# Paired diagonal turns, paired weight turns, and another order in the first units of a block, in the backward pass of a gated attention and feed-forward mix

## The chip, the core and the metric

The kernel runs on one core of a Trainium2 chip. The core has a matrix engine (TensorE, PE in the profile, with its weight loads shown as PEld), a vector engine (DVE), an activation engine (ACT), a general engine (POOL) and SyncE (SP), which here only issues DMAs. Each engine works through its own list of instructions in order and waits for the others on semaphores. Sixteen DMA engines move data between device memory and the on-chip memory, and they also turn (transpose) tiles on the way. The metric is the device time of one execution in microseconds (us). Three runs of the kernel before took 967.56, 969.1 and 969.56 us; the median is 969.1.

## The reference, cut to what matters

The forward pass mixes two branches with a gate per row. Branch A is attention with 32 heads of 16 columns over 2048 positions, in which each query sees itself and the 255 positions before it. Branch B is a gated feed-forward layer.

```python
qkv = (x @ wqkv).reshape(B, S, 3, H, Dh) ...          # S 2048, D 512, H 32, Dh 16
mask = (idx[:, None] - idx[None, :] >= 0) & (idx[:, None] - idx[None, :] < 256)
p = softmax(where(mask, q k^T * Dh ** -0.5, -1e9))
a = (p @ v) @ wo
b = ((x @ W_gate) * (x @ W_gate > 0) * (x @ W_up)) @ W_down        # F 1376
g = sigmoid((x * gate_w).sum(-1, keepdims=True))
out = g * a + (1 - g) * b
```

The kernel returns `out` and, for a given `grad_out`, the gradients of x, wqkv, wo, W_gate, W_up, W_down and gate_w, in bfloat16.

## The kernel before

The kernel has three stages. The first (0 to about 258 us) runs the feed-forward layer forward and backward and writes its intermediate results to device memory. The second (about 258 to 771 us) is attention, forward and backward. The third (to the end at 964 us) multiplies the stored results by turned weights and gives `out` and the gradient of x. The change touches the second stage, and the turned weights that the second stage loads for the third.

**Units.** The 32 heads are cut in four column chunks `c` of 128 columns, that is eight heads each. The 2048 positions are cut in 16 blocks of 128. For each chunk and each query block `j` the window reaches over the key blocks `j-2`, `j-1` and `j`. Such a pair of blocks is handled for four heads at a time (`half` 0 or 1), and that is one unit. A block has six units, block 0 has two and block 1 has four, so that there are 360 units in all. The role of a unit is `d` (diagonal, the key block is the query block), `m` (middle) or `f` (far). In a full block the order is m, f, d of the first half and then m, d, f of the second. The first unit of a block is thus an m unit of the first half, except in block 0.

**One unit.** `front` makes the scores ST on PE (L611), takes the exponential into `Pu` on ACT (L617) and masks it on POOL for d and f units (L619, L622). `front_dp` makes dPT on PE (L631), `gradp` multiplies it into `Pd` on DVE (L636). Three units later (`LAG = 3`) `rowsum` multiplies `Pu` and `Pd` into the accumulator BA on PE (L645, L647); after the last unit of a block ACT copies BA out (L651) and `small_ops` on DVE and POOL finish the block's rows. BA has one buffer. `flip` turns `Pu` and `Pd` into `p2`: d units and m units of the first half by a DMA that SyncE issues (L659), two units after `front`; the other units by eight PE transposes (L668) into PSUM and a copy by ACT or DVE in turn (L72, L74), three units after `front`. In the last chunk the last two blocks (`c == DC - 1`, `j >= NT - 2`) are turned by PE alone. `cd_piece` later multiplies the turned tiles by the finished rows into the accumulator CD (L486, L489), which ACT copies out (L492); these pieces wait in the list `cdq` with the number of the unit from which they may run.

**Order of the work.** The loop `while n <= NU + LAG` writes out the order by hand, one turn of the loop per unit `n`. PE gets ST of unit n, the row sums of unit n-3 (L820), the PE transposes of unit n-3, dPT of unit n (L836), one or two CD pieces (L838 to L840) and, where a running budget `credit` allows, a part of the next projections or of the gradient of wqkv. The scores, dPT, projections and weight gradients share four PSUM buffers (tag `M`). SyncE gets the turns of unit n-2, then weights, stores and the copies `z` that spread projected rows, in the order of the loop.

**Buffers.** `PP` (six buffers) holds `Pu` and `Pd` of a unit that is turned by DMA or is diagonal; `Pu` and `Pd` (four each) those of the other units. The turned tiles have seven buffers for d, seven for m and four for f.

**Turned weights.** `plan` lists what is loaded for the third stage while attention runs. `turns` gives one DMA for each 128 columns of wqkv, W_gate and W_up (`turn_w`, L516), 34 in all, and the loop issues one in every three units.

## Time and profile before

| | us |
|---|---|
| median of three runs | 969.1 |
| the profiled execution | 966.0 |
| its span, first to last instruction | 964.3 |
| 0 to 258, PE busy | 251.73 of 258 |
| 258 to 771, PE busy | 492.67 of 513 |
| the same stretch, DVE, ACT and POOL busy | 344.16, 353.56 and 336.21 |
| 771 to 964.3, PE busy | 187.78 of 193.3 |
| granted TensorE clock, mean | 0.993 |

The page gives busy times by engine, the chain of work that ended last, and groups of instructions by source line. A group's line reads: line, engine, operation, what it writes and reads, shape, number, busy time, mean duration in ns, idle time of the engine just before these instructions, and what ended that idle time. Matmuls are pipelined: each is drawn longer than the distance at which the next can start, so that short waits of PE do not show as idle time. A timeline shows instructions in order of time (start, duration, engine, line, operation). For a DMA the issue on its queue and the landing are told apart.

SyncE issues the DMA turns of attention as `DMA_TRANSPOSE` instructions. The turns of PP (128x1024 elements) land a median of 3.8 us after their issue, at least 3.0; the turns of the first stage's `hT` (128x512) a median of 2.8, at least 2.3. The seven large turns of the third stage land a median of 8.6 us after their issue.

### The profile page before, as it was taken

The numbers are of one execution on the slowest core, as the hardware profiler recorded it, in microseconds if no ns is written. First come the engines' busy times: TensorE is split into PE (matmuls) and PEld (weight loads), VectorE is DVE, ScalarE is ACT, GpSimd is POOL, SyncE is SP. The second block draws the span as 40 slices with busy tenths as digits, with TensorE's granted clock in tenths as the row PEclk, the third lists the DMA queues.
The fourth block names the chain that finished last, engine by engine and source line by source line (L and its number), as shares of the span: only waits on it lengthen the run. The fifth ranks groups of instructions, "written<-read, shape, count | busy, mean of one in ns | idle before, by whom it ended". The sixth has DMA issues, their size and how long they took to land.

```text
span 964.3 us, 27296 instructions
## 1 busy us (share of the span) xinstructions
PE 932.2 (97%) x11065; PEld 589.3 (61%) x11065; DVE 504.1 (52%) x921; ACT 457.8 (47%) x795; POOL 486.8 (50%) x935
## 2 busy tenths in 40 slices
PE   8999999999989999999999999979998999999998
PEld 5556556566557766677776776756766744444443
DVE  4433435334467776567775767756676432223223
ACT  5522322223367877667776677756676410000001
POOL 1645445455177667656676656755666521112211
PEclk9999999999999999999999999989999999999999
DMA  9988799999579797987979869998999699787741
GB/s 286 191 188 192 184 199 213 198 215 207 133 123 141 112 178 127 135 159 115 175 126 147 156 105 172 135 149 140 167 139 199 148 260 228 193 189 190 188 106 44
DMA packets 473399, 160.32 MB, mean 166 GB/s; under 512 B 402008, under 2 KB 470968, under 8 KB 473272
## 3 DMA queue, kind: packets, MB, share of 16 engines
q1 hardware_dynamic: 450872, 135.49, 76.6%
q10 hardware_dynamic: 20592, 17.84, 6.5%
q0 software_dynamic: 1808, 5.24, 1.6%
q8 instruction: 86, 1.41, 0.6%
q14 instruction: 41, 0.34, 0.2%
HBM read 32.15 MB, written 36.31 MB: 71 GB/s over the span
## 4 chain that ended last, share of the span: by engine, by line
PE 82%; POOL 5%; DMA 4%; DVE 4%; issue 2%; ACT 1%; SPq 1%; POOLq 0%; DVEq 0%; ACTq 0%
PE wps L371 7%; PE dxps L952 7%; PE pt L668 7%; PE ST L611 7%; PE dPT L631 7%; PE dxps L967 4%; PE wps L568 4%; PE BA L645 4%; PE pp L128 4%; PE dhps L324 4%; PE ups L324 4%; PE dps L373 4%; PE bps L921 3%; PE gps L324 3%; PE CD L486 3%
## 5 line engine op out<-in xcount | busy, mean ns | idle before, releaser
L636 DVE TENSOR_TENSOR PP<-PP,dPT 128x512 bf16<-128x512 bf16 x186 | 126.2, 681 | 51.5 <-POOL PP L619 46.4
L636 DVE TENSOR_TENSOR Pd<-Pu,dPT 128x512 bf16<-128x512 bf16 x174 | 118.0, 679 | 63.5 <-POOL Pu L622 47.9
L631 PE MATMUL dPT<-z,V 128*128 128x512 bf16 x360 | 137.1, 381 | 9.3 <-ACT PP L617 7.6
L617 ACT ACTIVATE PP<-ST 128x512 bf16<-128x512 f32 x186 | 112.0, 602 | 67.5 <-PE ST L611 50.7
L611 PE MATMUL ST<-z,K 128*128 128x512 bf16 x360 | 136.9, 380 | 4.8 <-DVE PP L636 1.4
L617 ACT ACTIVATE Pu<-ST 128x512 bf16<-128x512 f32 x174 | 105.3, 605 | 45.7 <-PE ST L611 35.9
L619 POOL TENSOR_SCALAR_AFFINE_SELECT PP<-PP 128x512 bf16<-128x512 bf16 x128 | 81.5, 637 | 79.2 <-ACT PP L617 78.3
L338 POOL TENSOR_TENSOR hT<-rg,upm 128x512 bf16<-128x512 bf16 x44 | 51.5, 1170 | 119.0 <-DVE upm L336 91.8
L486 PE MATMUL CD<-rq,p 128*128 128x32 bf16 x1440 | 109.6, 177 | 0.7 <-ACT rows_st L492 0.5
L489 PEld LDWEIGHTS <-p 128*128 128x128 bf16 x1440 | 86.3, 96 | 35.5 <-issue 2.4
L489 PE MATMUL CD<-rq,p 128*128 128x16 bf16 x1440 | 106.7, 169 | 0.0
L371 PE MATMUL wps<-dgu_r,x_r 128*128 128x256 bf16 x704 | 105.6, 273 | 0.4 <-DVE wst L74 0.4
L486 PEld LDWEIGHTS <-p 128*128 128x128 bf16 x1440 | 98.9, 96 | 10.7 <-issue 8.5
L72 ACT COPY p<-pt 128x1024 bf16<-128x1024 bf16 x89 | 90.7, 1019 | 4.8 <-PE pt L668 1.2
L371 PEld LDWEIGHTS <-x_r 128*128 128x128 bf16 x704 | 68.8, 98 | 31.7 <-issue 1.0
L622 POOL TENSOR_SCALAR_AFFINE_SELECT Pu<-Pu 128x512 bf16<-128x512 bf16 x112 | 71.2, 635 | 28.9 <-ACT Pu L617 27.3
L930 ACT COPY a_sb<-aps 128x512 f32<-128x512 f32 x16 | 9.4, 586 | 153.1 <-issue 137.6
L336 DVE SCALAR_TENSOR_TENSOR upm<-rg,ups 128x512 bf16<-128x512 bf16 x44 | 30.1, 684 | 80.0 <-PE ups L324 40.3
L330 ACT ACTIVATE rg<-gps 128x512 bf16<-128x512 f32 x44 | 26.3, 598 | 89.1 <-PE gps L324 44.1
L668 PE MATMUL pt<-ident,Pd 128*128 128x128 bf16 x696 | 67.8, 220 | 0.0
L668 PE MATMUL pt<-ident,Pu 128*128 128x128 bf16 x696 | 67.1, 218 | 0.1
L373 PE MATMUL dps<-db_r,h_r 128*128 128x512 bf16 x176 | 66.7, 379 | 0.0
(159 smaller groups left out, 2033.7 us busy)
## 6 DMA issues: line engine op xcount, KB each, us to landing
dqkvo_d<-rows_st SPq DMA_DIRECT2D x7, 1024.0 KB, 6.4
hT_d<-hT ACTq DMA_DIRECT2D x44, 128.0 KB, 2.3
dgT_d<-dgu ACTq DMA_DIRECT2D x44, 128.0 KB, 2.9
duT_d<-dgu ACTq DMA_DIRECT2D x44, 128.0 KB, 2.9
duT_g<-duT_d SPq DMA_DIRECT2D x8, 640.0 KB, 5.4
gt<-hT_d SPq DMA_DIRECT2D x7, 640.0 KB, 5.3
dgT_g<-dgT_d SPq DMA_DIRECT2D x7, 640.0 KB, 5.2
z<-zT SPq DMA_DIRECT2D x60, 64.0 KB, 2.2
```

Source lines behind the costliest of these rows:

```text
L72: nc.scalar.copy(out, in_)
L324: nc.tensor.matmul(out[:], lhsT=w(c), rhs=x(c), start=(c == 0), stop=(c == DC - 1))
L371: nc.tensor.matmul(acc["w"][:, c, :], lhsT=x_r[:, t, c * P:(c + 1) * P], rhs=k.dgu_r[:, :, i, :], start=(go_ and c % 2 == 0), stop=no_, sk ...
L373: nc.tensor.matmul(acc["d"][:], lhsT=k.h_r[:, i, :], rhs=db_r[:, t, :], start=go_, stop=no_)
L486: nc.tensor.matmul(cd[0][:, h, :], lhsT=p2[:, 0, hh, :], rhs=rq[:, h, 0:2 * Dh], start=cd[1], stop=True, skip_group_check=True)
L489: nc.tensor.matmul(cd[0][:, h, 0:Dh], lhsT=p2[:, 1, hh, :], rhs=rq[:, h, 2 * Dh:3 * Dh], start=False, stop=True, skip_group_check=True)
L611: nc.tensor.matmul(ST[:], lhsT=KTt[:, ksl], rhs=z[:, 0, jl, :, :], start=True, stop=True)
L617: nc.scalar.activation(u.Pu[:], ST[:], ACT.Exp)
L619: nc.gpsimd.affine_select(out=u.Pu[:], in_=u.Pu[:], compare_op=ALU.is_ge, fill=0.0, base=0, pattern=[[0, HH], [1, P]], channel_multiplier=-1)
L631: nc.tensor.matmul(u.dPT[:], lhsT=VTt[:, ksl], rhs=z[:, 1, jl, :, :], start=True, stop=True)
L636: nc.vector.tensor_tensor(out=u.Pd[:], in0=u.Pu[:], in1=u.dPT[:], op=ALU.mult)
L668: nc.tensor.transpose(pt[:, a, hh, :], src[:, hh, :], ident[:])
```

## The change

- The two diagonal units of a query block share one tile `PPd`, and after the second one a single DMA of 128x2048 elements turns both. Before, each had a DMA of its own, the first one two units after its own `front`.
- The buffers change with that: `PPd` has two buffers of double size and `PPm` three, in place of six of `PP`; `Pu` and `Pd` have three for four; the turned pairs `P2d` have four (of two units each) for seven of one, and the turned m tiles six for seven.
- The exception for the last two blocks of the last chunk is gone: their d units and the m units of the first half are turned by DMA too. That takes six of the 178 PE turns away and adds two pairs and two single DMA turns.
- Weights are turned two column blocks at a time, 18 DMAs in place of 34.
- In the loop turn in which the row sums of a block's first unit come up, PE gets dPT of unit n and the CD piece (or pieces) ahead of these row sums. In all other turns the order stays.

Counted over the program, SyncE issues 64 turns of pairs and 60 of single units in place of 182 turns, and 18 of weights in place of 34.

```diff
-        def turn_w(name, src, k, tag, at):
-            piece_of(name, k, tag, at)
-            r0 = min(k * P, src.shape[1] - P)
-            nc.sync.dma_start_transpose(out=W6[(name, k)], in_=src[:, r0:r0 + P])
+        def turn_w(name, src, ks, tag, at):
+            for i, k in enumerate(ks):
+                piece_of(name, k, tag, at + i)
+            r0 = min(ks[0] * P, src.shape[1] - len(ks) * P)
+            nc.sync.dma_start_transpose(out=W6[(tag, "t")][:, at:at + len(ks), :], in_=src[:, r0:r0 + len(ks) * P])
...
-                        u.dma = (u.role == "d" or (u.role == "m" and half == 0)) and (c < DC - 1 or j < NT - 2)
-                        u.wide = u.role == "d" or u.dma
+                        u.dma = u.role == "d" or (u.role == "m" and half == 0)
...
-            if u.wide:
-                u.PP = wk.tile([P, 2, HH, P], BF, tag="PP", bufs=6, name="PP")
+            if u.role == "d":
+                if u.half == 0:
+                    pairs[(u.c, u.j)] = wk.tile([P, 2, 2, HH, P], BF, tag="PPd", bufs=2, name="PPd")
+                u.PP = pairs[(u.c, u.j)][:, u.half, :, :, :]
+                u.Pu, u.Pd = u.PP[:, 0, :, :], u.PP[:, 1, :, :]
+            elif u.dma:
+                u.PP = wk.tile([P, 2, HH, P], BF, tag="PPm", bufs=3, name="PPm")
                 u.Pu, u.Pd = u.PP[:, 0, :, :], u.PP[:, 1, :, :]
             else:
-                u.Pu = wk.tile([P, HH, P], BF, tag="Pu", bufs=4, name="Pu")
+                u.Pu = wk.tile([P, HH, P], BF, tag="Pu", bufs=3, name="Pu")
...
         def flip(u):
+            if u.role == "d":
+                if u.half == 0:
+                    return
+                p2 = wk.tile([P, 2, 2, HH, P], BF, tag="P2d", bufs=4, name="p2d")
+                nc.sync.dma_start_transpose(out=p2[:].rearrange("p b a h q -> p (b a h) q"),
+                                            in_=pairs.pop((u.c, u.j))[:].rearrange("p b a h q -> p (b a h q)"))
...
+                return
             if u.dma:
-                p2 = wk.tile([P, 2, HH, P], BF, tag=f"P2{u.role}", bufs=7, name="p2")
+                p2 = wk.tile([P, 2, HH, P], BF, tag="P2m", bufs=6, name="p2")
...
-                if LAG <= n < NU + LAG:
-                    w = units[n - LAG]
-                    ahead = w.first and not w.dma
-                    if ahead:
-                        flip(w)
+                w = units[n - LAG] if LAG <= n < NU + LAG else None
+                if u is not None and w is not None and w.first:
+                    front_dp(u)
+                    pieces()
+                if w is not None:
                     rowsum(w)
-                    if not (w.dma or ahead):
+                    if not w.dma:
                         flip(w)
...
-                if u is not None:
+                if u is not None and not (w is not None and w.first):
                     front_dp(u)
...
+                if not (u is not None and w is not None and w.first):
+                    pieces()
```

`pieces()` holds the loop that ran CD pieces before (L838 to L841), word for word.

More of the change, by code (lines that the diff above doesn't have):

```diff
@@ L528, in turns @@
         def turns(name, src, k0, k1, tag):
-            return [lambda k=k: turn_w(name, src, k, tag, k - k0) for k in range(k0, min(k1, src.shape[1] // P + (src.shape[1] % P > 0)))]
+            full, end = src.shape[1] // P, -(-src.shape[1] // P)
+            ks = range(k0, min(k1, full))
+            sets = [list(ks[i:i + 2]) for i in range(0, len(ks), 2)] + ([[full]] if k0 <= full < min(k1, end) else [])
+            return [lambda s=s: turn_w(name, src, s, tag, s[0] - k0) for s in sets]
         def loads(name, src, k0, tag):
@@ L599 @@
                         u.role = ("d", "m", "f")[j - kb]
-                        u.dma = (u.role == "d" or (u.role == "m" and half == 0)) and (c < DC - 1 or j < NT - 2)
-                        u.wide = u.role == "d" or u.dma
+                        u.dma = u.role == "d" or (u.role == "m" and half == 0)
                         units.append(u)
         NU = len(units)
+        pairs = {}
         def front(u):
@@ L633, in gradp @@
         def gradp(u):
-            if not u.wide:
-                u.Pd = wk.tile([P, HH, P], BF, tag="Pd", bufs=4, name="Pd")
+            if not u.dma:
+                u.Pd = wk.tile([P, HH, P], BF, tag="Pd", bufs=3, name="Pd")
             nc.vector.tensor_tensor(out=u.Pd[:], in0=u.Pu[:], in1=u.dPT[:], op=ALU.mult)
@@ L656, in flip @@
         def flip(u):
+            if u.role == "d":
[4 more added lines that the diff above has]
+                                            in_=pairs.pop((u.c, u.j))[:].rearrange("p b a h q -> p (b a h q)"))
+                for b in range(2):
+                    P2[(u.c, u.j, u.kb, b)] = p2[:, b, :, :, :]
+                return
             if u.dma:
-                p2 = wk.tile([P, 2, HH, P], BF, tag=f"P2{u.role}", bufs=7, name="p2")
+                p2 = wk.tile([P, 2, HH, P], BF, tag="P2m", bufs=6, name="p2")
                 nc.sync.dma_start_transpose(out=p2[:].rearrange("p a h q -> p (a h) q"),
@@ L668, in flip @@
                     nc.tensor.transpose(pt[:, a, hh, :], src[:, hh, :], ident[:])
-            p2 = wk.tile([P, 2, HH, P], BF, tag=f"P2{u.role}", bufs={"d": 7, "m": 7, "f": 4}[u.role], name="p2")
+            p2 = wk.tile([P, 2, HH, P], BF, tag=f"P2{u.role}", bufs={"m": 6, "f": 4}[u.role], name="p2")
             evac(p2[:], pt[:], eng)
@@ L781, in background, with pieces @@
                 return more
+            def pieces():
+                nonlocal credit
+                for _ in range(2 if len(cdq) > 6 or (len(cdq) > 1 and cdq[1][5] and cdq[1][0] <= n and cdq[1][2] < NT - 1) else 1):
+                    if cdq and cdq[0][0] <= n:
+                        cd_piece(*cdq.pop(0)[1:])
+                        credit -= 0.2
             while n <= NU + LAG or ev or cdq or bgq:
@@ L834 @@
                                     cdq.append((e, w.c, kb, qb, half, qb == qbs[-1] and half == 1))
-                if u is not None:
+                if u is not None and not (w is not None and w.first):
                     front_dp(u)
                 credit += SLOT - 0.63 - (0.44 if LAG <= n < NU + LAG and not units[n - LAG].dma else 0.0)
-                for _ in range(2 if len(cdq) > 6 or (len(cdq) > 1 and cdq[1][5] and cdq[1][0] <= n and cdq[1][2] < NT - 1) else 1):
-                    if cdq and cdq[0][0] <= n:
-                        cd_piece(*cdq.pop(0)[1:])
-                        credit -= 0.2
+                if not (u is not None and w is not None and w.first):
+                    pieces()
                 if n >= NU:
```

## The prediction

> **What bounds the kernel now.** I read the page's busy times and its chain first, then the span in three stretches (0 to 258 us feed-forward, to 771 attention, then the last matmul stage), then the attention stretch in TensorE's timeline, the waits, and SyncE's queue. The diff touches the attention stretch alone (513.0 us, of which PE is busy 492.7).

> ```profile
> PE 932.2 (97%) x11065; PEld 589.3 (61%) x11065; DVE 504.1 (52%) x921; ACT 457.8 (47%) x795; POOL 486.8 (50%) x935
> PE 82%; POOL 5%; DMA 4%; DVE 4%; issue 2%; ACT 1%; SPq 1%; POOLq 0%; DVEq 0%; ACTq 0%
> ```

> PE sets the pace, in its program's order, so a gain must come from PE having fewer instructions or waiting less. Its waits are the next view (engine, what waited for what: us, times, longest):

> ```profile
> PE dPT L631 <- ACT PP L617: 7.6, 5, 3.3
> PE pp L131 <- DVE zT L140: 3.0, 7, 0.4
> PE BA L645 <- ACT BAs L651: 3.0, 8, 1.1
> ```

> That understates the row sums. A 512-column matmul is drawn 0.38 us long, but what follows it starts 0.215 us after it when nothing waits. In an ordinary block:

> ```profile
> 305.06 0.38 PE L631 MATMUL dPT<-z,V 128*128 128x512 bf16 x1
> 305.27 0.38 PE L611 MATMUL ST<-z,K 128*128 128x512 bf16 x1
> 305.68 0.18 PE L645 MATMUL BA<-KV,PP 128*128 128x33 bf16 x1
> ...
> 305.88 0.38 PE L631 MATMUL dPT<-z,V 128*128 128x512 bf16 x1
> 306.10 0.18 PE L486 MATMUL CD<-rq,p 128*128 128x32 bf16 x1
> ```

> ```profile
> 304.64 0.60 ACT L617 ACTIVATE PP<-ST 128x512 bf16<-128x512 f32 x1
> 305.13 0.50 ACT L651 COPY BAs<-BA 128x400 f32<-128x400 f32 x1
> ```

> dPT to the next ST is 0.21 (305.06 to 305.27), but ST to BA is 0.41: BA has one buffer, and ACT copies out the last block's sums until 305.63. PE loses 0.19 there, most of it hidden in the drawn length. Taken so in all 64 blocks of the timeline, start of BA less start of ST less 0.215 adds up to 11.5 us, in 48 of them, mostly 0.15 to 0.20; six are over 0.42 (0.82, 0.44, 0.47, 1.25, 0.45, 0.51).

> The other loss is a late DMA. The chain, in order of time, in two stretches:

> ```profile
> 637.96 4.62 DMA p<-PP
> ```

> ```profile
> 714.36 4.40 DMA p<-PP
> ...
> 728.65 6.73 DMA p<-PP
> ```

> Each time ACT's exponential waited for a PP buffer that a turn had still to read, and the dPT row above (7.6 us, 5 times, all from 635 to 737 us) is what PE lost. The turns were late because SyncE issued without a pause:

> ```profile
> 623.38 1.26 SPq L659 DMA_TRANSPOSE p<-PP  x1
> 624.69 1.32 SPq L516 DMA_TRANSPOSE d<-in_B_W_gate_dram  x1
> 626.11 2.64 SPq L659 DMA_TRANSPOSE p<-PP  x2
> 628.81 1.33 SPq L516 DMA_TRANSPOSE d<-in_B_W_gate_dram  x1
> 630.23 2.24 SPq L659 DMA_TRANSPOSE p<-PP  x1
> ```

> **Step 1, dPT and a CD piece ahead of first row sums.** Nothing is added. dPT (0.215) and eight CD matmuls (306.10 to 306.30, 0.20) stand before BA, so up to 0.415 us of each wait is covered: 11.5 less what the six long ones keep (0.40 + 0.02 + 0.05 + 0.83 + 0.03 + 0.09 = 1.4) is 10.1. Early blocks without CD pieces cover less, and at 265.90 us dPT itself waits for DVE until 267.15, as it would at 510 and 637. I take **-8.5**; bounds -10 and 0, and rival C for worse. CD pieces read turns that are two blocks old, and behind the moved BA only that unit's own sums are queued, needed six units later.

> **Step 2, fewer issues on SyncE.** What an issue costs depends little on size in these rows (min/median/max ns):

> ```profile
> L352 SPq DMA_TRANSPOSE h_r<-hT x44: 1188/1204/3940, 15.4 to 232.6; - x44
> ```

> ```profile
> L659 SPq DMA_TRANSPOSE p<-PP x182: 1231/1285/4414, 257.7 to 749.8; - x182
> ```

> ```profile
> L759 SPq DMA_TRANSPOSE gt<-dqkvo_d x7: 5234/6456/6877, 790.4 to 915.8; - x7
> ```

> h_r is half of a PP turn, and doubling adds 0.04 to 0.08 us. A pair (128x2048) is in no row: from below 1.33 (one more such step), from above 2 x 1.285 = 2.57 by size, or 3.2 as half of gt, which stands behind 640 KB loads. PP is the nearest row, so I take 1.6. Queue time before: 182 turns x 1.285 + 34 weights x 1.27 = 277 us of 513. After: 64 pairs x 1.6 + 60 singles x 1.285 + 18 weights x 1.35 (the 128K-element "early" turns took 1.32 to 1.66) = 204. That is 73 us less, and the weights (16 fewer) leave exactly the stretches where SyncE never paused. From 655 to 745 us SyncE would hold 11 pairs, 10 singles, about 6 weight turns, 4 early turns, 2 row turns and some 22 plain loads and stores of 0.6: 60 us of 90. So the late turns should go: **-8** (7.6 and what the drawn lengths hide), bounds 0 and -9. DMA bytes are unchanged.

> [...]

> **Step 3, two pair buffers.** A pair's turn is issued only when its second unit is ready, and block j+2 writes the same buffer. Landing took at least 2.3 us for h_r and 3.0 for PP, so a pair takes about 3.0 + 2 x 0.7 = 4.4. Inside a chunk there are 8 units (about 11.6 us) between, and it is hidden. Where a column chunk starts, blocks 0 and 1 have 2 and 4 units and the turn stands behind the row turn and two z copies: in chunk 1 at 382.93 it would land at 387.3, while block 2's diagonal exponential stood at 383.78; in chunk 2, 507.55 lands at 512.0 against 509.91; I put chunk 3 like chunk 2. These are 3.5, 2.1 and 2.1 us of ACT waiting. PE goes on for about 1.7 us of it (the four M buffers take the next ST, dPT and ST), which leaves 1.8 + 0.4 + 0.4, taken as **+3**, bounds +1 and +11 (landing at 9.3 us, the slowest gt, four times the data). Late next would be the block's CD pieces, but those come two blocks later.

> **Step 4, the last two blocks turned by DMA.** Six PE turns go. One is 0.45 us of PE (742.54 to 742.99 in the timeline), so **-2.7**; PE waits for almost nothing from 745 to 772 us (busy 26.44 of 27). Six copies go too (three ACT 1.0, three DVE 0.68), both engines having room. The added turns stand among weight loads and a 640 KB load that lands after 6.1 us, but the CD pieces that need them come behind 10.0 us of weight-gradient matmuls. With that cover gone it would cost up to 3 us. Bounds -2.7 and 0.

> **Step 5, smaller changes** (Pu, Pd three buffers for four, P2m six for seven): Pu and Pd are freed three units after use and wanted six later; P2m leaves three units. Nothing, bound +1.

> **Sum:** -8.5 - 8 + 3 - 2.7 = -16.2 on the profiled 966.0 us (span 964.3 and 1.7 around it), so 949.8. The median of the runs shown is 3.1 higher, so **952.9, said as 953**. Worst and best of its own terms: about -5 and -22, which is 964 to 947.

> **Rivals.**
> A, issue by size: pairs hold SyncE 2.57 each, the queue gains only 11 us (weights), a third of the late turns goes and they land later. -8.5 - 2.5 + 5 - 2.7 = -8.7, so 960. For it: gt's long issue. Against: h_r beside PP. Chance 0.17.
> B, the row-sum wait only changes place, since ACT also frees the CD bank (L492) and the M buffers in those units: step 1 gives 2. -9.7, so 959. Against: ACT is busy 69% of the stretch, and L492 cost PE 0.5 in all. Chance 0.12.
> C, slower: the moved dPT waits for DVE's product of the unit two before, whose dPT held the M buffer four back. At 713.05 (ST) that product ends at 713.88, 0.62 us after dPT could start, so the block would end 0.24 later than now (a wait of 0.62 for BA's 0.38, and nothing stands ahead to cover it). Over 61 blocks that is +14.6 instead of -8.5: +6.9 in all, so 976. It decides from about 43 of 61 blocks on. Against: in the built program's order the moved dPT names ACT in 54 of 64 blocks and DVE in 10. Chance 0.11.
> D, the pair buffers bind everywhere: landing near 9 us uses up the 11.6 us inside chunks wherever SyncE is 3 us late. -8.5 + 11 - 2.7, no step 2: 969, no change. Chance 0.06.

> **Numbers.** Mine 0.54. Faster than 0.2% (2 us, what a measurement here can tell) is mine, A and B less a few hundredths: 0.81; within it 0.05; slower 0.14. The range goes from 944 to 967: it holds mine, A and B with their bounds and leaves C and part of D out.

> **What would show it.** Right: BA starts 0.43 or more after its ST with dPT and CD between and no gap; the wait of dPT for PP's exponential falls from 7.6 to under 2 with none after 650 us; pairs issue in 1.3 to 1.8 us. Wrong: a pair's issue near 2.6, dPT waiting for DVE in the first units, or exponentials waiting for the pairs' turns in every chunk. A slower result would overturn step 1 or step 3, whichever of these rows grew.

## The result, and the profile after

The changed kernel takes 971.8 us (median of 8 runs, 969.75 to 973.15) beside 968.4 us for the kernel before on the same chip (8 runs, 967.24 to 971.41): ratio 1.0031, 95% interval 1.0017 to 1.0045. It is 0.3% slower, 3.0 us, where 16 us less were predicted. The profiled execution took 972.45 us (span 970.7), 6.45 more than that of the kernel before, so the two traces lie further apart than the medians.

The busy times and the chain on the page of the changed kernel:

```profile
PE 928.5 (96%) x11017; PEld 588.2 (61%) x11017; DVE 501.0 (52%) x918; ACT 456.6 (47%) x792; POOL 487.0 (50%) x935
PE 69%; DMA 10%; POOL 7%; DVE 6%; ACT 3%; issue 3%; SPq 1%; POOLq 0%; ACTq 0%; DVEq 0%
```

TensorE has less to do (928.5 us for 932.2) in a longer span, and DMA's share of the chain has gone from 4% to 10%. TensorE's waits in the attention stretch (us, times, longest), then those of ScalarE for a turn, in the kernel before and in the changed one:

```profile
PE dPT L641 <- ACT PPd L627: 10.8, 6, 3.8
PE ST L616 <- ACT PPd L627: 2.5, 2, 2.1
PE dPT L641 <- DVE Pd L646: 2.3, 2, 1.4
PE BA L655 <- ACT BAs L661: 2.2, 1, 2.2
```

```profile
ACT PP L617 <- DMA p<-PP: 11.5, 6, 3.9
```

```profile
ACT PPd L627 <- DMA p2d<-PPd: 19.1, 8, 4.0
```

The old late-turn wait of dPT (7.6 us) has not gone: it is 10.8 us, now for PPd. ScalarE's wait for turns rose from 11.5 to 19.1 us. The row sums, on the other hand, look as the reordering meant them to, here in the same block as before the change (timeline of TensorE, lines left out between):

```profile
304.44 0.38 PE L616 MATMUL ST<-z,K 128*128 128x512 bf16 x1
304.65 0.38 PE L641 MATMUL dPT<-z,V 128*128 128x512 bf16 x1
304.87 0.18 PE L486 MATMUL CD<-rq,p2d 128*128 128x32 bf16 x1
...
305.07 0.18 PE L655 MATMUL BA<-KV,PPm 128*128 128x33 bf16 x1
```

BA starts 0.63 us after its ST with dPT and a CD piece between, and nothing stands still. ScalarE's eight waits for a pair are between 0.35 and 4.03 us long. The one in chunk 1 (SyncE's, ScalarE's and TensorE's timelines; in brackets the idle time before an instruction and what ended it) looks so:

```profile
379.54 1.45 SPq L171 DMA_TRANSPOSE rows<-zT  x1
381.08 1.25 SPq L468 DMA_DIRECT2D z<-zT  x2
382.42 2.15 SPq L671 DMA_TRANSPOSE p2d<-PPd  x1
```

```profile
383.20 0.37 ACT L492 CAST rows_st<-CD 128x256 bf16<-128x256 f32 x1 [0.59 <-PE CD L489]
386.97 0.60 ACT L627 ACTIVATE PPd<-ST 128x512 bf16<-128x512 f32 x1 [3.40 <-DMA p2d<-PPd]
387.46 0.49 ACT L661 COPY BAs<-BA 128x400 f32<-128x400 f32 x1
```

```profile
383.85 0.38 PE L616 MATMUL ST<-z,K 128*128 128x512 bf16 x1
387.62 0.59 PE L641 MATMUL dPT<-z,V 128*128 128x512 bf16 x1 [3.39 <-ACT PPd L627]
```

Block 0's pair was complete at 376.1 us (end of its second product), but its turn was issued at 382.42, behind the row turn and two z copies, and landed at 386.87. More than half of that delay is not SyncE's own work: from 373.19 to 379.54 it issued nothing, and the row turn, next in its list, went out 0.03 us after POOL had ended `rq` (L714), which reads the rows. The pairs of block 0 in chunks 2 and 3 stood behind the row turn in the same way (it went out at 508.55 and 640.94, again 0.03 us after `rq`). Block 2's exponential, which writes the same buffer, stood still for 3.40 us. TensorE stood still for 3.39: ScalarE's whole wait reached it. There is a second loss. The table by windows (us, busy of each engine with its instructions, PEclk = granted TensorE clock) around that stall:

```profile
382.00:385.90 3.90, 2.23 (x48) 1.59 (x45) 2.74 (x5) 0.97 (x2) 3.73 (x10) 1.00 0.83 155
385.90:392.70 6.80, 5.08 (x76) 3.43 (x76) 2.05 (x4) 3.96 (x7) 3.91 (x10) 0.50 1.09 165
392.70:396.00 3.30, 3.30 (x54) 2.30 (x51) 1.88 (x3) 1.59 (x4) 1.98 (x5) 1.00 0.97 184
```

For 6.8 us from 385.9 on, in the middle of the wait, the granted clock is 0.5. In the attention stretch of the kernel before there were two such windows, 10.2 us in all, at its two long waits (from 641.1 and 736.7 us; the first is shown); in the changed kernel there are five, 23.8 us.

```profile
641.10:647.90 6.80, 4.58 (x63) 3.04 (x63) 2.13 (x4) 3.19 (x6) 3.21 (x7) 0.50 0.94 154
```

Where a matmul starts is read from the timeline: over these windows the starts lie further apart than the same pairs of lines do at full clock (stalls over 0.6 us left out) by 7.6 us in the changed kernel and by about 3 in the one before.

### The profile page after: what moved, and what is told of

The parts are those of the page before. It is cut to its first block, busy times and chain, and to the rows that moved or that the text cites. A ratio compares the mean times of both kernels' runs of the same rounds, so it can differ in the third digit from the quotient of the medians.

```text
span 970.7 us, 26875 instructions
## 1 busy us (share of the span) xinstructions
PE 928.5 (96%) x11017; PEld 588.2 (61%) x11017; DVE 501.0 (52%) x918; ACT 456.6 (47%) x792; POOL 487.0 (50%) x935
## 4 chain that ended last, share of the span: by engine, by line
PE 69%; DMA 10%; POOL 7%; DVE 6%; ACT 3%; issue 3%; SPq 1%; POOLq 0%; ACTq 0%; DVEq 0%
PE dxps L976 7%; PE wps L371 6%; PE ST L616 6%; PE pt L687 5%; PE dPT L641 5%; PE wps L572 4%; PE dxps L991 4%; DMA p2d<-PPd 4%; PE pp L128 4%; PE bps L945 3%; PE dhps L324 3%; PE dps L373 3%; PE ups L324 3%; PE gps L324 3%; PE BA L655 3%
## 5 line engine op out<-in xcount | busy, mean ns | idle before, releaser
L641 PE MATMUL dPT<-z,V 128*128 128x512 bf16 x360 | 138.6, 385 | 13.9 <-ACT PPd L627 10.8
L629 POOL TENSOR_SCALAR_AFFINE_SELECT PPd<-PPd 128x512 bf16<-128x512 bf16 x128 | 81.6, 637 | 85.9 <-ACT PPd L627 85.5
L646 DVE TENSOR_TENSOR PPd<-PPd,dPT 128x512 bf16<-128x512 bf16 x128 | 87.5, 683 | 56.5 <-POOL PPd L629 55.0
L627 ACT ACTIVATE PPd<-ST 128x512 bf16<-128x512 f32 x128 | 77.1, 602 | 51.3 <-PE ST L616 28.9
L72 ACT COPY p<-pt 128x1024 bf16<-128x1024 bf16 x86 | 87.6, 1019 | 4.8 <-PE pt L687 2.4
L486 PE MATMUL CD<-rq,p 128*128 128x32 bf16 x928 | 68.4, 177 | 0.0
L687 PE MATMUL pt<-ident,Pd 128*128 128x128 bf16 x688 | 67.8, 222 | 0.0
L687 PE MATMUL pt<-ident,Pu 128*128 128x128 bf16 x688 | 67.2, 220 | 0.0
L489 PEld LDWEIGHTS <-p 128*128 128x128 bf16 x928 | 54.8, 96 | 20.2 <-issue 1.1
L489 PE MATMUL CD<-rq,p 128*128 128x16 bf16 x928 | 66.7, 169 | 0.0
L486 PEld LDWEIGHTS <-p 128*128 128x128 bf16 x928 | 62.1, 96 | 1.2 <-issue 1.1
```

The lines of the kernel that those rows point to most:

```text
L72: nc.scalar.copy(out, in_)
L486: nc.tensor.matmul(cd[0][:, h, :], lhsT=p2[:, 0, hh, :], rhs=rq[:, h, 0:2 * Dh], start=cd[1], stop=True, skip_group_check=True)
L489: nc.tensor.matmul(cd[0][:, h, 0:Dh], lhsT=p2[:, 1, hh, :], rhs=rq[:, h, 2 * Dh:3 * Dh], start=False, stop=True, skip_group_check=True)
L627: nc.scalar.activation(u.Pu[:], ST[:], ACT.Exp)
L629: nc.gpsimd.affine_select(out=u.Pu[:], in_=u.Pu[:], compare_op=ALU.is_ge, fill=0.0, base=0, pattern=[[0, HH], [1, P]], channel_multiplier=-1)
L641: nc.tensor.matmul(u.dPT[:], lhsT=VTt[:, ksl], rhs=z[:, 1, jl, :, :], start=True, stop=True)
```

## The experiments

All ratios are to the kernel before, run on the same chip. 1% is 9.7 us. The last column is read from the one profiled execution of each kernel.

| kernel | parts of the change in it | ratio, 95% interval | half-clock us in attention |
|---|---|---|---|
| changed | all | 1.0031 (1.0017 to 1.0045) | 23.8 |
| order_only | reordering | 0.9999 (0.9984 to 1.0014) | 17.0 |
| weights_only | weight pairs | 0.9907 (0.9885 to 0.9929) | 0 |
| pairs_only | diagonal pairs, tail by DMA | 1.0098 (1.0079 to 1.0118) | 20.4 |
| ring3 | all, three pair buffers | 0.9875 (0.9856 to 0.9894) | 3.4 |
| order_weights | reordering, weight pairs | 0.9867 (0.9846 to 0.9889) | 0 |
| weights_tail | weight pairs, tail by DMA | 0.9882 (0.9861 to 0.9904) | 0 |
| order_weights_tail | all but the diagonal pairs and their buffers | 0.9872 (0.9852 to 0.9893) | 0 |
| ring3_no_order | ring3 without reordering | 0.9892 (0.9871 to 0.9913) | 3.4 |
| halves | all, but a turn for each diagonal unit | 0.9968 (0.9949 to 0.9986) | 10.2 |
| tail_on_pe | all but the tail | 1.0051 (1.0036 to 1.0066) | 23.8 |
| ring3_from4 | ring3, reordering from block 4 on | 0.9859 (0.9837 to 0.9881) | 0 |

Where the time goes is read from the start of each block's first ST, less that of the kernel before (us, column chunk and block):

| block | changed | order_only | weights_only | pairs_only | ring3 |
|---|---|---|---|---|---|
| (0,0) | -0.5 | -1.0 | -1.0 | -0.9 | -0.4 |
| (1,2) | -0.1 | -1.4 | -1.0 | +0.3 | -0.8 |
| (1,4) | +2.8 | -1.7 | -1.0 | +3.3 | -1.0 |
| (2,4) | +6.5 | -1.5 | -1.0 | +7.8 | -0.8 |
| (3,4) | +6.4 | -2.0 | -5.3 | +9.1 | -6.3 |
| (3,12) | +5.0 | -1.8 | -6.4 | +8.0 | -7.8 |
| (3,15) | +5.3 | +0.8 | -10.4 | +8.5 | -12.7 |

The first row, block (0,0), lies ahead of all that the edits touch. What it shows was there before, so a step is read as the difference of two rows.

### The parts alone, and a third buffer

**order_only**: the kernel before with the diff's last three hunks, in short

```diff
+                if u is not None and w is not None and w.first:
+                    front_dp(u)
+                    pieces()
                 if w is not None:
...
                     rowsum(w)
```

> The kernel before with the reordering alone (the current unit's dPT and one CD piece ahead of the first row sums of a block). Theory T (the loss of the whole change comes from the two pair buffers): the reordering by itself still gains, about 4 us rather than the 8.5 predicted, since the changed kernel's blocks gained 0.05 to 0.15 us each where no pair bound: 963 to 966 us, and the row sums' waits for ScalarE's copy BAs drop from 11.5 us to under 3. Rival O (the reordering itself costs, because the moved dPT or the later row sums make something else late): at or above the kernel before, 968 us or more, with dPT waits that the kernel before has not.

Measured: 965.39 us beside 965.87, no change. Rival O's total came true, though not simply for its reason. TensorE's waits:

```profile
PE dPT L631 <- ACT PP L617: 10.7, 6, 4.2
PE pp L131 <- DVE zT L140: 3.0, 7, 0.4
PE dPT L631 <- DVE Pd L636: 2.3, 2, 1.4
```

BA's waits are gone from the list, and the blocks of chunks 1 and 2 run 1.4 to 2.5 us ahead of those of the kernel before, of which 1.0 was there at block (0,0). In chunk 3 the late turns take it back (10.7 us of dPT waits for 7.6): by (3,15) the kernel is 0.8 us behind. The moved dPT also waits for VectorE's product (2.3 us), once for 1.38 us up to 509.64, with a half-clock window from 510.0 to 513.4 us behind it.

**weights_only**: the kernel before with the new turn_w and turns.

> The kernel before with the weights' column blocks turned two at a time, nothing else. Theory T: nearly nothing, 0 to -2 us, since these turns lie in the last chunk and the tail, where the queue's lateness cost 7.6 us in dPT waits together with the singles; what falls is the dPT wait for ACT PP. Rival W (a paired weight turn holds the queue or its destination longer and delays the block turns behind it): +1 to +4 us, with longer waits for PP from chunk 3 on.

Measured: 956.97 us, ratio 0.9907, 9.0 us less; both theories missed. The longest of TensorE's waits in attention are then

```profile
PE pp L131 <- DVE zT L140: 2.6, 6, 0.4
PE BA L649 <- ACT BAs L655: 2.6, 8, 0.7
PE dPT L635 <- DVE PP L640: 1.5, 3, 0.6
```

dPT no longer waits for PP's exponential, the clock is 1.0 throughout, and the table shows the gain where the weights' turns lie: from -1.0 at (2,4) to -5.3 at (3,4), and from -6.4 to -10.4 in the last blocks. Eighteen weight turns for 34 did by themselves all that step 2 hoped for, where theory T had 2 us at most.

**pairs_only**: the changed kernel with the reordering and the weight pairs taken back.

> The changed kernel with the reordering and the weight pairs taken back: both diagonal units of a block in one pair tile, two such buffers, one turn, the last blocks by DMA too. Theory T: all of the loss is here and none of the gain of the reordering: 973 to 981 us, 5 to 13 above the kernel before, with exponentials waiting for the turn of a pair at the starts of chunks 1, 2 and 3 and in the tail. Rival W or O (the loss is made by the other parts): 964 to 970 us.

Measured: 975.41 us, 9.5 above the kernel before, as theory T said. Without the reordering the same stalls appear under another name:

```profile
PE BA L651 <- ACT BAs L657: 19.9, 13, 4.3
```

The copy BAs is not slow (0.49 us in the changed kernel's timeline above); it stands on ScalarE behind the exponential that waits for a pair's buffer. That is how one late turn reaches TensorE by two roads.

**ring3**:

```diff
-                    pairs[(u.c, u.j)] = wk.tile([P, 2, 2, HH, P], BF, tag="PPd", bufs=2, name="PPd")
+                    pairs[(u.c, u.j)] = wk.tile([P, 2, 2, HH, P], BF, tag="PPd", bufs=3, name="PPd")
...
-                p2 = wk.tile([P, 2, 2, HH, P], BF, tag="P2d", bufs=4, name="p2d")
+                p2 = wk.tile([P, 2, 2, HH, P], BF, tag="P2d", bufs=3, name="p2d")
```

> The changed kernel with three buffers for the untransposed pairs in place of two, and three in place of four for the turned ones (the same memory). Theory T: the waits of exponentials for a pair's turn go, and with them the matmul clock's drops that followed: 958 to 964 us, 8 to 13 below the changed kernel. Rival L (the pair's turn issues late and lands late whatever buffers there are, and the late one is then the CD piece that reads the turned pair): within 2 us of the changed kernel, 970 to 973 us, with CD pieces waiting for DMA p2d. Rival M (three turned pairs are too few): turns wait for CD pieces, 968 to 975 us.

Measured: 953.27 us, ratio 0.9875, 15.1 us less than the changed kernel by the ratios, with the same instructions and the same memory. The pairs' turns issue and land as before (first the changed kernel, then ring3; SyncE's times in ns, min/median/max):

```profile
L671 SPq DMA_TRANSPOSE p2d<-PPd x64: 1322/2233/4404, 260.7 to 764.5; - x64
...
DMA to landing us min/median/max: 4.3/5.3/7.8
```

```profile
L671 SPq DMA_TRANSPOSE p2d<-PPd x64: 1317/2090/3822, 260.9 to 751.7; - x64
...
DMA to landing us min/median/max: 4.2/5.1/7.5
```

ScalarE waits for no pair any more, so rivals L and M fall: the turns are as late as they were, and nobody needs them sooner. Theory T had 8 to 13 us, so it is right in kind and a little low. What is left is the moved dPT's 1.38 us behind VectorE at 510 us with 3.4 us at half clock.

### Combinations

**order_weights** joins the two edits.

> The kernel before with the reordering and the weight pairs, every diagonal unit still turned by itself from six PP buffers. In the profile of the reordering alone the blocks ran 2.4 us ahead of the kernel before until the middle of chunk 3 and lost it there to dPT waits for late turns (6.6 us against 3.9 us). Theory Q (the reordering gains some 2.4 us, and the late turns took it): with the weights paired it stays, 2 to 3 us below the weight pairs alone, ratio to the kernel before about 0.988. Rival N (the reordering gains nothing in the end, since its dPT waits for VectorE's product in other places, 1.38 us at 509 us with a drop of the matmul clock behind it): within 1 us of the weight pairs alone, ratio 0.990 to 0.992.

**weights_tail** adds to the weight pairs

```diff
-                        u.dma = (u.role == "d" or (u.role == "m" and half == 0)) and (c < DC - 1 or j < NT - 2)
+                        u.dma = u.role == "d" or (u.role == "m" and half == 0)
```

> The kernel before with the weight pairs, and the last two blocks' diagonal and middle units turned by DMA one at a time instead of on TensorE. The predicted step: 2.7 us below the weight pairs alone, ratio about 0.988. Rival H (the turns in the tail are late, and exponentials or CD pieces wait for them): ratio 0.990 to 0.994, with dPT or CD waits after 740 us that the weight pairs alone do not have.

**ring3_no_order** is ring3 with the reordering taken back.

> The kernel with three pair buffers and three turned pairs, but the reordering taken back: weight pairs, diagonal pairs, last blocks by DMA. Theory P (the diagonal pairs give nothing of themselves once the weights are paired; what the three-buffer kernel has over the weight pairs alone is the reordering and the tail): at the level of the weight pairs with the DMA tail, within 1 us, ratio 0.988 to 0.991. Rival G (fewer turns on the queue are worth some us more): 2 us or more below that kernel.

Measured: 954.64, 955.78 and 956.92 us beside 967.43; ratios 0.9867, 0.9882 and 0.9892. The intervals are 2 us to each side, so of differences this small only the direction is given. The reordering takes 0.0040 off the weight pairs and 0.0017 off the three-buffer kernel; in the traces of order_weights and weights_only it is worth 2.7 us between the first block and block (3,13), and in the block after that 1.9 of them are lost, to two waits of dPT for late turns (2.0 us). Theory Q fits better than N, although N's waits are there too:

```profile
PE dPT L635 <- DVE Pd L640: 2.6, 3, 1.4
PE dPT L635 <- DVE PP L640: 2.1, 7, 0.6
PE dPT L635 <- ACT PP L621: 2.0, 2, 1.2
```

In the kernel with weight pairs alone these three were 0.9, 1.5 and none: what BA no longer waits, dPT partly does. The tail's step (0.0025 below the weight pairs) agrees with the 2.7 us predicted, but in the profiled executions of the two the last wait before a CD piece ends at 759.98 and 759.77 us, only 0.2 apart, so it is not settled. Theory P fits the pairs: ring3_no_order is within 1.1 us of weights_tail, where it had said 1.

### What a stall costs

**stalls**: the weight pairs alone, and ahead of the first exponential of four blocks

```diff
+            if u.first:
+                for _ in range({(1, 5): 4, (1, 12): 6, (2, 5): 8, (2, 12): 11}.get((u.c, u.j), 0)):
+                    nc.scalar.copy(idle[:], idle[:])
             nc.scalar.activation(u.Pu[:], ST[:], ACT.Exp)
```

> The kernel with the weight pairs alone (granted clock 1.0 through its attention stage), with 4, 6, 8 and 11 copies of a spare 128x512 tile on ScalarE ahead of the first exponential of blocks (1,5), (1,12), (2,5) and (2,12): about 2.4, 3.6, 4.8 and 6.6 us of ScalarE. TensorE has about 1.7 us of cover there. Theory K (a stall of TensorE of some 2 to 3 us brings windows of 3.4 us at half the granted clock right behind it): blocks later by 0.7, 1.9, 3.1 and 4.9 us for the stalls alone, and by 1.7 to 3.4 us more at each of the longer two or three, 16 to 20 us in all, with the clock's records at 0.5 there. Rival (the drops in clock seen in the other kernels are not made by the stalls): about 10.6 us in all and no record below 1.0 at those places.

Measured (one execution, 966.99 us): a copy took 617 ns, so ScalarE was held for 2.5, 3.7, 4.9 and 6.8 us, and against the trace of the weight pairs alone the blocks came 0.6, 1.6, 3.9 and 5.9 us later, 12.0 in all. The third stall and what follows it, in TensorE's timeline, and the clock:

```profile
540.22 0.58 PE L617 MATMUL ST<-z,K 128*128 128x512 bf16 x1 [2.46 <-ACT PP L626]
```

```profile
532.00:539.70 7.70, 5.76 (x103) 4.04 (x101) 3.77 (x6) 6.27 (x12) 4.15 (x10) 1.00 0.55 106
539.70:543.10 3.40, 2.88 (x21) 1.79 (x21) 1.48 (x3) 3.01 (x6) 1.27 (x2) 0.50 0.71 135
543.10:550.00 6.90, 6.90 (x113) 4.83 (x112) 5.84 (x13) 4.17 (x7) 4.00 (x12) 1.00 0.54 67
```

The kernel that these four edits were made to has no half-clock window in this stage; this one has one that begins in the 2.46 us gap, 0.5 us before it ends, and another (6.8 us, from 601.1) in the 3.33 us gap that ended at 603.83, and none at the two short stalls. Theory K is right in kind: the stalls make the windows. It is too high in price: 12.0 us and not 16 to 20. The 1.2 us that the third stall adds to the second on ScalarE cost 2.3 us, so the window costs about 1.1 us.

### Depth or size, the tail, and the best version

**halves** keeps the two pair buffers and turns each half as soon as it is ready:

```diff
                 if u.half == 0:
-                    return
...
+                    turned[(u.c, u.j)] = wk.tile([P, 2, 2, HH, P], BF, tag="P2d", bufs=4, name="p2d")
+                p2 = turned[(u.c, u.j)][:, u.half, :, :, :]
+                nc.sync.dma_start_transpose(out=p2.rearrange("p a h q -> p (a h) q"),
+                                            in_=u.PP.rearrange("p a h q -> p (a h q)"))
```

> The changed kernel with its two pair buffers kept, but each diagonal unit turned by a DMA of its own as soon as it is ready (64 more issues on the queue, each of about 1.25 us, landing in 3.8 in place of 5.3 us). Theory D (the depth of two is what binds: a buffer is free only when its second unit is turned, which is then little earlier than before): 964 to 972 us, 0 to 6 below the changed kernel, exponentials still waiting for turns at the chunks' starts. Rival E (the paired turn itself, its late issue and long landing, is the loss, and two buffers would do): at the level of the reordering with weight pairs and the DMA tail, 953 to 957 us.

**tail_on_pe** puts the changed kernel's last two blocks back on TensorE (the old condition on u.dma, a PE turn for diagonal units there).

> The changed kernel with the turns of the last two blocks' diagonal and middle units back on TensorE. In the changed kernel the last block's first ST lost 4.3 us in the block before it, to a pair's turn that was 6 us late with a half-clock window behind it, and three buffers took that away. Theory T (the tail's turns by DMA are a loss only while the pair buffers are two): 967 to 970 us, 2 to 5 below the changed kernel. Rival (the tail is a gain in the changed kernel too, as predicted): 973 to 976 us.

**order_weights_tail** is all but the diagonal pairs.

> The kernel before with all parts of the change but the diagonal pairs: reordering, weight pairs, last blocks by DMA one unit at a time. Theory Q (diagonal pairs in three buffers still give the queue some slack in the last chunk, where the reordering without them lost 2 us to late turns at 726 to 731 us): 953 to 956 us, 1 to 3 above the three-buffer kernel. Rival P (diagonal pairs are worth nothing): at or below the three-buffer kernel, ratio 0.985 to 0.988.

**ring3_from4** is ring3 with `w.first and u.j >= 4` as the condition of the reordering.

> The three-buffer kernel with the reordering only in blocks 4 to 15 of a chunk. In the three-buffer kernel the moved dPT waited 1.38 us for VectorE's product at 510 us, in block (2,2), with 3.4 us at half clock behind it, and blocks 1 of each chunk lost 0.2 to 0.3 us. Theory C (the moved dPT costs where VectorE is late, in the first blocks of a chunk): 1.5 to 2.5 us below the three-buffer kernel, ratio to the kernel before 0.985 to 0.986, granted clock 1.0. Rival (that wait lies before the reordered slot or moves elsewhere): within 0.7 us of it, ratio 0.987 to 0.988.

Measured, beside 967.25 us: halves 964.6, tail_on_pe 972.37, order_weights_tail 955.13, ring3_from4 953.64.

- halves: 6.1 us below the changed kernel, 9.3 above order_weights_tail. Theory D: turns of 3.8 us in place of 5.3 still leave this wait, eight times:

```profile
ACT PPd L628 <- DMA p2d<-PPd: 14.6, 8, 4.0
```

  The depth binds; the longer turn of a pair adds to it.
- tail_on_pe: 1.0051, 0.2% above the changed kernel. Theory T fell. The 4.2 us stall at 751.86 is there as in the changed kernel (3.77 at 750.62): it comes from the pair of block (3,12), which is turned by DMA in both. The tail by DMA is a small gain or nothing everywhere.
- order_weights_tail against ring3: 0.9872 and 0.9875. The diagonal pairs give nothing that this measurement can tell, even with the third buffer; neither theory's full 1 to 3 us shows.
- ring3_from4: 951.6 us of span for ring3's 953.1, no half-clock window in attention, ratio 0.9859 for 0.9875. The direction is that of theory C, the intervals overlap. The window is a weak argument for it: ring3_no_order has one at 514.5 us without any moved dPT, and order_weights and order_weights_tail have the same wait (1.39 and 1.38 us) and no window; the last section sets two such waits side by side. It is the lowest ratio found, 1.4% under the kernel before, with order_weights at 0.9867 not told apart from it.

## Why the prediction was wrong

The ratios add up when the parts are put on one after the other (1.0 to 0.9907, 0.9867, 0.9872, 1.0031, times 968 us; each step is known to about 3 us, the last to 2.4):

| step of the prediction | predicted | measured |
|---|---|---|
| 2, fewer issues: the weight pairs | -8 with the diagonal pairs | -9.0 |
| 1, reordering | -8.5 | -3.9 (0 without the weight pairs) |
| 4, last blocks by DMA | -2.7 | +0.5 (-2.4 without the reordering) |
| 3 and 5, diagonal pairs in two buffers, smaller rings | +3 | +15.4 |
| sum | -16.2 | +3.0 |

**Step 3 failed**, and it is 12.4 of the 19 us. The mechanism had been named, and it is the one that came: at the start of chunk 1 the exponential's wait was put at 3.5 us and was 3.40. What was mis-sized:
- How often. Three waits of 7.7 us in all were counted; there were eight of 19.1. "Inside a chunk 8 units (about 11.6 us) ... it is hidden" held for most blocks, but not in the weights' stretch (3.27 us at 632.78, the first block of chunk 3, with the turn at 627.34 issued 4.5 us late) and not in the tail (4.03 at 749.98, 6.0 late). Chunk 2's wait was 3.73 us for 2.1, chunk 3's 2.23 for 2.1. A pair landed 5.3 us after its issue, where 4.4 was taken.
- The cover. "PE goes on for about 1.7 us of it" was not so: 3.40 us on ScalarE were 3.39 on TensorE. ScalarE's wait began at 383.57 and TensorE's last ST started at 383.85; the dPT after it then waited for the delayed exponential itself, which ended at 387.57. In other places it is the copy BAs, behind the exponential in ScalarE's queue, that TensorE waits for (2.2 us here, 19.9 in pairs_only).
- The clock. No term of the sum had it: 7.6 us lost in half-clock windows, about 3 before. The windows at 641.1 and 736.7 us were in the trace of before, at the very waits that step 2 was about.

Rival D had the cause (pair buffers that bind) and came closest, 969 for 971.8, but by a landing of 9 us everywhere, which did not occur (4.3 to 7.8 us); the lateness on SyncE did it, at the chunks' starts and in two stretches. The third buffer, which changes no turn and no instruction of another engine, shows the cause: it takes 15.1 us off.

**Step 1** was right in what it does to BA (the example above; BA's waits leave the list in order_only) and too large in what that is worth: 1.6 to 3.9 us by the two ratios, not 8.5. In chunk 0 the unit in which the order changes became 0.19 us shorter (median of blocks 4 to 14, order_only against before), just as the step said, but the first unit of every second block became 0.16 to 0.29 us longer; in blocks 6, 10 and 14 its dPT starts 0.37 us after the instruction ahead of it instead of 0.17, waiting for VectorE's product. In chunks 1 and 2 the gain was 0.10 and 0.15 us a block and mostly stayed; in chunk 3 the late turns took more than it gave. So rival B, "the row-sum wait only changes place", is the better account for a part of the blocks, and for another reason than ScalarE's other copies. Rival C's mechanism is there too, in a few places (2.3 us in two waits), far from 43 blocks.

**Step 2** came out at its size, but all of it from the 16 weight turns less, and the agreement is partly luck, because the relief that it was summed from did not come. The pairs issue in 2.23 us (median; mean 2.50), not 1.6, and 64 of them hold SyncE for 160 us. All turns and weights of the attention stretch hold it for 287 us where they held it for 322, which is 35 us less and not 73. Rival A's 2.57 us was near the mean, but its rule "by size", by which a pair takes twice as long, does not fit the shortest issues: 1.32 us for a pair beside 1.23 for half the size. The mean (2.50 beside 1.50 for the single turns before, 1.7 times as long) lies between. What makes the median 0.9 us longer than the shortest was not tried. The prediction's sign that the dPT wait falls under 2 us holds for the weight pairs alone, not for the whole change.

**Steps 4 and 5**: the tail's -2.7 lies within what the three comparisons allow (-2.4, +0.5, and -1.9 against tail_on_pe); step 5 was not separated from step 3, but ring3 keeps its smaller Pu, Pd and P2m and stands level with order_weights_tail, so it costs nothing that shows.

## What to carry to other kernels

When transfers are put together, the buffer they leave is held from the first part written until the whole has landed (here until 386.87 us, 0.10 before the exponential that wrote it next): count the ring's depth in these units against the shortest stretch of the loop (here a chunk's first blocks, of 2 and 4 units in place of 6) and against the queue's worst lateness, not its mean. Take the queue's relief from transfers that nobody waits for: 16 fewer weight turns gave 9 us, 64 fewer turns on the critical ring gave nothing. And a wait that is removed in one place is worth what the next wait on that engine leaves of it: read what the instruction behind it will wait for.

## What the runs showed of the hardware

A stall of TensorE can cost more than its length: in the stalls run the third stall held ScalarE for 1.2 us more than the second and cost 2.3 us more. In TensorE's waits of 2.1 to 3.8 us in the attention stretch of the kernel before and of the changed one, or up to 1.6 us after them, the granted clock fell to 0.5 for 3.4 or 6.8 us; in order_only it did so 0.35 us after the wait of 1.38. In the changed kernel's window from 385.9 us (the timeline of TensorE):

```profile
388.50 0.58 PE L616 MATMUL ST<-z,K 128*128 128x512 bf16 x1
388.88 0.23 PE L655 MATMUL BA<-KV,Pu 128*128 128x33 bf16 x1
...
389.14 0.59 PE L687 MATMUL pt<-ident,Pu 128*128 128x128 bf16 x4
389.52 0.63 PE L687 MATMUL pt<-ident,Pd 128*128 128x128 bf16 x4
389.95 0.63 PE L641 MATMUL dPT<-z,V 128*128 128x512 bf16 x1
390.38 0.23 PE L486 MATMUL CD<-rq,p 128*128 128x32 bf16 x1
```

From dPT to the next start are 0.43 us, twice the 0.215 at full clock, while the narrow matmuls still start 0.027 us apart (0.025). The matmuls of 128 columns (L687) pay too: four of them take 0.38 and 0.43 us from start to start here, and 0.22 at full clock (from 305.73 us). Counted by the starts as above, the single windows of 3.4 us cost 1.2 to 1.5 us in the changed kernel and 1.4 in the one before, about 1.1 in the stalls run; those of 6.8 us, with a part of a stall inside, 1.7 to 1.8. The wide matmuls pay, the narrow ones hardly.

```profile
506.58:509.99 3.41, 1.91 (x40) 1.11 (x37) 1.31 (x3) 2.44 (x5) 3.25 (x9) 1.00 0.95 124
509.99:513.40 3.41, 3.41 (x61) 2.55 (x58) 2.55 (x5) 1.13 (x3) 2.79 (x8) 0.50 1.25 194
```

```profile
506.93:510.34 3.41, 2.35 (x47) 1.55 (x44) 1.71 (x4) 3.18 (x6) 3.33 (x9) 1.00 0.93 124
510.34:513.75 3.41, 2.97 (x70) 2.37 (x70) 2.35 (x5) 1.28 (x3) 2.71 (x8) 1.00 1.08 160
```

In order_only the whole wait lies in one step, which is idle for 1.50 us, and the next is at half clock. In order_weights a border cuts the wait, the two steps are idle for 1.06 and 0.44 us, and none follows at half clock. So in these two runs the same wait came with a window or without one by where it fell. The 1.5 us are what these traces show; no run tried the border itself.
